# Attention scores of a fused recurrence, mixture and MLP kernel: three split products or one plain fp32 product

## The chip, the core and the metric

The kernel runs on one core of one Trainium2 chip. A core has a matmul engine (TensorE, PE in the profile; its loading of the stationary operand is listed apart as PEld), a vector engine (VectorE, DVE), an engine for activations (ScalarE, ACT), a general engine (GpSimd, POOL) and one that only issues transfers (SyncE, SP). They run side by side, each through its own list of instructions in order, and wait for each other by semaphores. SBUF is the working memory with 128 rows (partitions); matmul results go to PSUM, which has eight banks per partition. The metric is the time of one execution on the device in microseconds; the median of three runs is given.

## The reference

Three stages on a batch of 4 sequences of 768 positions. First a gated linear recurrence with 8 heads of 48:

```
state = alpha[:, :, t, :, None] * state + einsum('bhd,bhe->bhde', k[:, :, t], v[:, :, t])
y[:, :, t] = einsum('bhd,bhde->bhe', q[:, :, t], state)
```

Then causal attention with four experts, of which each position uses the two with the largest gate:

```
for e in range(E):                        # E = 4, Hd = 64
    q = x @ wq[e]; k = x @ wk[e]; v = x @ wv[e]
    scores = 1.0 / np.sqrt(Hd) * (q @ k.transpose(0, 2, 1))
    scores = np.where(causal, -1000000000.0, scores)
    a = softmax(scores)
    out += gate weight of e * (a @ v @ wo[e])
```

Last a layer norm and an MLP of width 384 to 1536 to 384 with a residual: `x + relu(xn @ w_ch1) @ w_ch2`. All in fp32. The weights of queries and keys are large (scaled by 23), so scores need many correct digits.

## The kernel before

**Numbers.** Two kinds of float are used on TensorE. A plain fp32 tile (F32) is multiplied by an instruction pair: one matmul call leaves two records in the trace. A tile of type FR (float32r) is multiplied by one record per call, with fewer digits. Where the kernel needs fp32 accuracy with FR tiles, it splits a value in a high part, rounded to FR by a ScalarE copy, and a low part, the rest, made on VectorE, and adds three products: high by high, low by high and high by low. The projections (line 304, 318), the output projection (505) and the MLP (631, 648) do so, and so do the attention scores (432). The recurrence (lines 221, 230, 244, 263), the transposes of the softmax (464) and the sums over values (487, 490) use plain fp32 operands.

**Stages.** `front()` walks over 24 chunks of 128 positions (6 per sequence): `gla_a`, `gla_b` and `gla_c` compute the recurrence, and after every second chunk `qkv(m)` projects 256 positions to queries, keys, values and gates. For queries and keys its matmuls fill a bank P with two row blocks of 128 x 256 (experts 0 and 1 in block 0, experts 2 and 3 in block 1, 64 rows each). The attention consists of 48 units (b, i, p): sequence b, query tile i of 128 positions, expert pair p. `scores(u)` makes the scores of the two experts of a pair (called heads here, h = 0 and 1) into PSUM, takes the row maximum (VectorE, line 438 and 440) and the exponential (ScalarE, line 442). Head h uses rows 64h to 64h+63 of TensorE's array, so that the two heads' matmuls are on different row tiles. A unit has 128 (i + 1) keys; above 512 it is worked in two halves of equal width, each with a bank per head. `transp(u)` transposes the exponentials, `av(u)` multiplies by the values, `wout` by the output weights. `back()` is the MLP in 12 blocks.

**Order.** The main loop goes over the units, makes scores two units ahead (LA = 2) and fills the gaps with steps of `front()` for sequences 0 to 2 and of `back()` for sequence 3, by tables of expected costs. The framework then orders each engine's list by its own schedule, so that one changed instruction can shift others. PSUM tiles are all named F and come from one pool of eight banks, handed out in turn.

**What is stored.** `new_gen(b)` makes, for even and odd b, four FR tiles of 128 x 2 x 768 (QH, QL, KH, KL: high and low parts of queries and keys) and the values V and gate weights W. The lines that the change touches are the copies after the projection (307 to 311) and the matmuls in `scores`:

```
for x in range(npc):
    for n, (qt, kt) in enumerate(((QH, KH), (QL, KH), (QH, KL))):
        for h in range(2):
            pe.matmul(P[h][x], qt[rs[h], p, qs], kt[rs[h], p, pw * x:pw * x + pw], ...)
```

Of the kernel before, what the change touches and what calls it, by code (L numbers as in the profile page):

```python
# [10 lines left out]
F32 = mybir.dt.float32  # L11
FR = mybir.dt.float32r
# [3 lines left out]
AF = mybir.ActivationFunctionType  # L16
OP = mybir.AluOpType
# [38 lines left out]
B, H, S, D = 4, 8, 768, 48  # L56
# [10 lines left out]
def f(ap):  # L67
    return ap.bitcast(F32)
# [3 lines left out]
def kernel(ctx: ExitStack, tc: tile.TileContext, akq, vd, wqkv, wo, g_ln, w1, w2, out):  # L72
    nc = tc.nc
    pe, dve, act, pool, sp = nc.tensor, nc.vector, nc.scalar, nc.gpsimd, nc.sync
# [21 lines left out]
    def psf():  # L96
        return psF.tile([128, 512], F32, tag="F", name="F")
# [16 lines left out]
    def new_gen(b):  # L114
        p = gen_pool[b % 2]
        if (b % 2, "t") not in GEN:
            GEN[b % 2, "t"] = (*(p.tile([128, 2, S], FR, name=f"{n}{b % 2}") for n in ("QH", "QL", "KH", "KL")),
                               p.tile([128, NSC, E * HD + E], F32, name=f"V{b % 2}"),
                               p.tile([128, NSC, E], F32, name=f"W{b % 2}"))
        GEN[b] = GEN[b % 2, "t"]  # L120
# [5 lines left out]
    GEN = {}  # L126
    wraw = []
    for k in range(KT):
        t = aw.tile([128, 772], F32, name="A", bufs=NA)
# [10 lines left out]
    for _ in range(NWU // 4):  # L140
        P = psf()
# [148 lines left out]
    def qkv(m):  # L290
        b, w = divmod(m, 3)
        if w == 0:
            new_gen(b)
        QH, QL, KH, KL, V, W = GEN[b]
        xh, xl = XT.pop(m)
        ts = slice(256 * w, 256 * w + 256)
        for mt in range(4):
            if mt % 2 == 0:
                P = psf().rearrange("p (x t) -> p x t", x=2)
            n = 0  # L300
            cs = slice(128 * mt, 128 * mt + 128)
            for wt, x in ((WH, xh), (WL, xh), (WH, xl)):
                for k in range(KT):
                    pe.matmul(P[:, mt % 2], wt[:, k, cs], x[:, k], start=(n == 0), stop=(n == 8))  # L304
                    n += 1
            if mt == 1:
                act.activation(QH[:, :, ts], P, AF.Copy, scale=0.125)
                dve.scalar_tensor_tensor(QL[:, :, ts], P, 0.125, f(QH[:, :, ts]), op0=OP.mult, op1=OP.subtract)
            elif mt == 3:
                act.activation(KH[:, :, ts], P, AF.Copy)  # L310
                dve.tensor_tensor(KL[:, :, ts], P, f(KH[:, :, ts]), op=OP.subtract)
            yield 980
        for t in range(2):
            P = psf()[:, :260]
            n = 0
            for wt, x in ((WH, xh), (WL, xh), (WH, xl)):
                for k in range(KT):
                    pe.matmul(P, x[:, k, 128 * t:128 * t + 128], wt[:, k, 512:772], start=(n == 0), stop=(n == 8))  # L318
                    n += 1
            act.activation(V[:, 2 * w + t], P, AF.Copy)  # L320
            yield 1000
        lg = V[:, 2 * w:2 * w + 2, 256:260]
        mx = sm.tile([128, 2, 1], F32, name="mx")
        dve.tensor_reduce(mx, lg, axis=AX.X, op=OP.max)
        l2 = sm.tile([128, 2, 4], F32, name="l2")
        pool.tensor_tensor(l2, lg, mx.to_broadcast([128, 2, 4]), op=OP.subtract)
        ex = sm.tile([128, 2, 4], F32, name="ex")
        act.activation(ex, l2, AF.Exp)
        rank = sm.tile([128, 2, 4], F32, name="rank")
        l_o = lg[:, :, None, :].to_broadcast([128, 2, 4, 4])  # L330
        l_s = lg[:, :, :, None].to_broadcast([128, 2, 4, 4])
        gt_ = sm.tile([128, 2, 4, 4], F32, name="gt_")
        eq_ = sm.tile([128, 2, 4, 4], F32, name="eq_")
        dve.tensor_tensor(gt_, l_o, l_s, op=OP.is_gt)
        dve.tensor_tensor(eq_, l_o, l_s, op=OP.is_equal)
        pool.tensor_tensor(eq_, eq_, tri[:, None].to_broadcast([128, 2, 4, 4]), op=OP.mult)
        pool.tensor_tensor(gt_, gt_, eq_, op=OP.add)
        dve.tensor_reduce(rank, gt_, axis=AX.X, op=OP.add)
        dve.scalar_tensor_tensor(ex, rank, 1.5, ex, op0=OP.is_lt, op1=OP.mult)
        sd = sm.tile([128, 2, 1], F32, name="sd")  # L340
        dve.tensor_reduce(sd, ex, axis=AX.X, op=OP.add)
        dve.tensor_scalar(sd, sd, 1e-9, None, op0=OP.add)
        dve.reciprocal(sd, sd)
        dve.tensor_tensor(W[:, 2 * w:2 * w + 2], ex, sd.to_broadcast([128, 2, 4]), op=OP.mult)
        yield 0
# [65 lines left out]

    def scores(u):
        b, i, p = UN[u]
        QH, QL, KH, KL, V, W = GEN[b]
        nk = 128 * (i + 1)
        qs = slice(128 * i, 128 * i + 128)
        nm = sm.tile([128, 2], F32, name="nm")
        den = sm.tile([128, 2], F32, name="den")
        M["nm"] = nm
        A = [aw.tile([128, 772], F32, name="A", bufs=NA) for _ in range(2)]  # L420
        wide = nk > 512
        pw = nk // 2 if wide else nk
        P = [[psf()[:, :pw] for x in range(1 + wide)] for h in range(2)]
        if wide:
            mx2 = sm.tile([128, 2], F32, name="mx2")
            dn2 = sm.tile([128, 2, 2], F32, name="dn2")
        npc = 1 + wide
        rs = [slice(64 * h, 64 * h + 64) for h in range(2)]
        for x in range(npc):
            for n, (qt, kt) in enumerate(((QH, KH), (QL, KH), (QH, KL))):  # L430
                for h in range(2):
                    pe.matmul(P[h][x], qt[rs[h], p, qs], kt[rs[h], p, pw * x:pw * x + pw], start=(n == 0), stop=(n == 2),  # L432
                              skip_group_check=True)
        for h in range(2):
            for x, t in enumerate(P[h]):
                m = mx2[:, h:h + 1] if x < npc - 1 else nm[:, h:h + 1]
                if x < npc - 1:
                    dve.tensor_reduce(m, t, axis=AX.X, op=OP.max, negate=True)
                else:
                    dve.tensor_tensor_reduce(t, t, cmask[:, 512 - pw:], -1.0, mx2[:, h:h + 1] if wide else 3e38, OP.add, OP.min, m)  # L440
            for x, t in enumerate(P[h]):
                act.activation(A[h][:, pw * x:pw * x + pw], t, AF.Exp, bias=nm[:, h:h + 1], scale=1.0 if x < npc - 1 else -1.0,  # L442
                               accum_out=dn2[:, h, x:x + 1] if wide else den[:, h:h + 1])
        AA[u] = A
        if wide:
            dve.scalar_tensor_tensor(den, dn2[:, :, 0], 1e-9, dn2[:, :, 1], op0=OP.add, op1=OP.add)
        else:
            dve.tensor_scalar(den, den, 1e-9, None, op0=OP.add)
        dve.reciprocal(den, den)
        rr = sm.tile([128, 2], F32, name="rr")  # L450
        pool.tensor_tensor(rr, den, W[:, i, 2 * p:2 * p + 2], op=OP.mult)
        RR[u] = rr
# [18 lines left out]

    def av(u):
        b, i, p = UN[u]
        V = GEN[b][4]
        if p == 0:
            OT[u // 2] = (aw.tile([128, 2, 128], FR, name="oh", bufs=2), aw.tile([128, 2, 128], FR, name="ol", bufs=2))
        oh, ol = OT[u // 2]
        P = psf()
        rr = RR.pop(u)
        at = ATT.pop(u)  # L480
        O = P[:, 128:256]
        with tc.manual_schedule(engines={mybir.EngineType.PE}):
            for x in range(i + 1):
                for h in range(2):
                    e = 2 * p + h
                    c = 128 * (h * (i + 1) + x)
                    pe.matmul(O[64 * h:64 * h + 64, :], V[:, x, HD * e:HD * e + HD], at[:, c:c + 128],  # L487
                              start=(x == 0), stop=(x == i), skip_group_check=True)
            for h in range(2):
                pe.matmul(P[64 * h:64 * h + 64, :128], rr[:, h:h + 1].to_broadcast([128, 64]), ident, start=True, stop=True,  # L490
                          skip_group_check=True)
        rb = aw.tile([128, 128], F32, name="rb", bufs=2)
        act.activation(rb, P[:, :128], AF.Copy)
        dve.tensor_tensor(rb, O, rb, op=OP.mult)  # L494
        act.activation(oh[:, p], rb, AF.Copy)
        (dve if OLE else pool).tensor_tensor(ol[:, p], rb, f(oh[:, p]), op=OP.subtract)
# [215 lines left out]
    for u in range(LA):  # L712
        scores(u)
    for u in range(nu):
        b, i, p = UN[u]
# [18 lines left out]
        else:  # L734
            nc2 = min(NC2, (u - u3) * CR // 2)
            while prog["cv"] < NC1 + nc2:
                n = prog["cv"]
# [84 lines left out]
```

## Time and profile before

| what | value |
|---|---|
| median of 3 runs | 748.21 us (744.76, 748.21, 753.51) |
| span of the profiled execution | 749.8 us |
| its mean granted TensorE clock | 0.97 of full speed |
| busy: TensorE, its weight loads | 713.5 us, 643.2 us |
| busy: VectorE, ScalarE, GpSimd | 447.5 us, 308.5 us, 174.5 us |
| records of the score matmuls (line 432) | 384, busy 51.2 us |

No time of the profiled execution apart from its span is given, so the span stands for it; it lies 1.6 us above the median. Busy is the time in which an engine had at least one instruction under way. Records of TensorE overlap, so its busy time, and the duration of one record, is more than what one instruction costs in a row of many; that is read from the distance between starts. The program has three parts that matter here: to about 60 us it starts up, from 60 to 360 us recurrence, projections and attention are mixed, from 360 to 462 us the attention of the last sequence is mixed with the MLP, and the rest is MLP alone.

### The profile page before, as it was taken

The page shows a single profiled execution, that of the slowest core. Times are in us where ns is not written, and L with a number is a line of the kernel's source. Part 1 is how long each engine was busy: PE and PEld are TensorE (multiplying, and loading weights), DVE is VectorE, ACT ScalarE, POOL GpSimd, SP SyncE. Part 2 cuts the span into 40 slices and gives each one's busy share as a digit, 9 for nine tenths or more (in the row PEclk, how much of TensorE's full clock was granted, in tenths as well). Part 3 has the DMA queues.
Part 4 walks back from the last instruction along what each step waited for, and adds up shares of the span by engine and source line. Part 5 has one row for each costly group of instructions (what it writes and reads, how often), then busy time and mean ns, then how long its engine had stood idle before and what let it go on. Part 6 is the DMA issues. An engine that isn't in the chain of part 4 may idle for free.

```text
span 749.8 us, 16242 instructions
## 1 busy us (share of the span) xinstructions
PE 713.5 (95%) x6520; PEld 643.2 (86%) x6520; DVE 447.5 (60%) x1241; ACT 308.5 (41%) x879; POOL 174.5 (23%) x284
## 2 busy tenths in 40 slices
PE   7599799989989999999899999999999999999998
PEld 6488678868868788779678888999999999999997
DVE  6757787767897787766678954254245335433521
ACT  3324455545555555555567545232223123212310
POOL 4624345243464334321223221000000000000000
PEclk8688999999999999999999999999999999999999
DMA  8113424233322622211932311001100100110100
GB/s 338 71 57 115 151 68 138 98 117 121 121 97 96 208 61 83 77 41 54 323 99 79 96 43 55 22 32 43 43 11 33 43 22 22 43 43 12 32 22 22
DMA packets 30427, 60.87 MB, mean 81 GB/s; under 512 B 2960, under 2 KB 19856, under 8 KB 30352
## 3 DMA queue, kind: packets, MB, share of 16 engines
q1 hardware_dynamic: 18864, 45.68, 18.3%
q10 hardware_dynamic: 8352, 9.44, 3.6%
q0 software_dynamic: 3136, 4.72, 2.3%
q8 instruction: 51, 0.84, 0.5%
q14 instruction: 24, 0.20, 0.1%
HBM read 45.67 MB, written 14.16 MB: 80 GB/s over the span
## 4 chain that ended last, share of the span: by engine, by line
PE 69%; DVE 9%; DMA 7%; ACT 4%; POOL 3%; issue 3%; SPq 0%; ACTq 0%; POOLq 0%; DVEq 0%
PE F L631 21%; PE F L648 20%; PE F L304 5%; PE F L487 5%; PE F L432 4%; PE F L464 3%; DMA ld<-in_akq_dram 3%; PE F L505 2%; DMA raw<-in_w_dram 2%; DVE gt L199 2%; PE F L263 2%; PE F L318 2%; PE F L221 1%; ACT A L442 1%; PE F L244 1%
## 5 line engine op out<-in xcount | busy, mean ns | idle before, releaser
L635 ACT ACTIVATE hh<-F 128x256 fp32r<-128x256 f32 x144 | 55.0, 384 | 196.6 <-PE F L631 196.0
L631 PE MATMUL F<-nh,w1hl 128*128 128x256 f32 x864 | 129.0, 284 | 0.0
L631 PEld LDWEIGHTS F<-nh,w1hl 128*128 128x128 f32 x864 | 114.4, 191 | 1.7 <-issue 0.7
L648 PE MATMUL F<-w2h,hh 128*128 128x384 f32 x288 | 98.8, 343 | 0.0
L648 PE MATMUL F<-w2l,hh 128*128 128x384 f32 x288 | 97.0, 337 | 0.0
L648 PE MATMUL F<-w2h,hl 128*128 128x384 f32 x288 | 96.9, 336 | 0.0
L636 DVE SCALAR_TENSOR_TENSOR hl<-F,hh 128x256 fp32r<-128x256 f32 x144 | 60.1, 419 | 56.8 <-ACT hh L635 56.3
L442 ACT ACTIVATE A<-F,nm 128x384 f32<-128x384 f32 (+4 forms) x128 | 68.4, 541 | 52.7 <-DVE nm L440 44.4
L652 DVE TENSOR_TENSOR xt<-F,xt 128x384 f32<-128x384 f32 x24 | 13.4, 558 | 110.5 <-PE F L648 110.5
L631 PE MATMUL F<-nl,w1hl 128*128 128x256 f32 x432 | 75.5, 283 | 0.0
L487 PE MATMUL F<-at,V 128*64 128x128 f32 x672 | 62.1, 286 | 2.3 <-ACT at L467 1.6
L631 PEld LDWEIGHTS F<-nl,w1hl 128*128 128x128 f32 x432 | 62.2, 192 | 0.2 <-issue 0.2
L487 PEld LDWEIGHTS F<-at,V 128*64 128x64 f32 x672 | 41.5, 137 | 19.1 <-issue 7.5
L464 PE MATMUL F<-ident,A 128*128 128x128 f32 x336 | 54.5, 284 | 3.3 <-DVE rb L494 2.6
L648 PEld LDWEIGHTS F<-w2h,hh 128*128 128x128 f32 x288 | 54.2, 188 | 1.1 <-issue 0.8
L648 PEld LDWEIGHTS F<-w2l,hh 128*128 128x128 f32 x288 | 54.2, 188 | 0.2
L648 PEld LDWEIGHTS F<-w2h,hl 128*128 128x128 f32 x288 | 54.1, 188 | 0.2 <-issue 0.2
L464 PEld LDWEIGHTS F<-ident,A 128*128 128x128 f32 x336 | 37.9, 142 | 12.6 <-issue 5.0
L221 PE MATMUL F<-ld 48*128 48x128 f32 x384 | 37.8, 309 | 9.1 <-issue 5.1
L221 PEld LDWEIGHTS F<-ld 48*128 48x128 f32 x384 | 30.2, 203 | 15.4 <-issue 9.8
L206 POOL TENSOR_TENSOR ld<-ld,gt 128x512 f32<-128x512 f32 (+1 forms) x26 | 30.2, 1166 | 56.4 <-DVE gt L199 29.1
L467 ACT ACTIVATE at<-F 128x512 f32<-128x512 f32 (+1 forms) x72 | 38.7, 542 | 6.6 <-PE F L464 4.8
(185 smaller groups left out, 1420.9 us busy)
## 6 DMA issues: line engine op xcount, KB each, us to landing
ld<-in_akq_dram SPq DMA_DIRECT2D x24, 770.0 KB, 4.8
vb<-in_vd_dram SPq DMA_DIRECT2D x24, 256.0 KB, 2.8
raw<-in_w_dram SPq DMA_DIRECT2D x18, 256.0 KB, 2.7
wsc<-whl ACTq DMA_DIRECT2D x18, 256.0 KB, 2.4
xs<-xo ACTq DMA_DIRECT2D x24, 192.0 KB, 1.9
w1hl<-wsc POOLq DMA_DIRECT2D x4, 1152.0 KB, 14.9
xt<-xs SPq DMA_DIRECT2D x24, 192.0 KB, 2.5
raw<-in_w_dram SPq DMA_DIRECT2D x12, 384.0 KB, 3.2
```

What stands on the lines that cost most here:

```text
L206: (dve if GQ else pool).tensor_tensor(q[:, js], q[:, js], gt[:, js, 1:], op=OP.mult)
L221: pe.matmul(P[h][:, j], k[r, j], q[r, j], start=True, stop=True)
L304: pe.matmul(P[:, mt % 2], wt[:, k, cs], x[:, k], start=(n == 0), stop=(n == 8))
L432: pe.matmul(P[h][x], qt[rs[h], p, qs], kt[rs[h], p, pw * x:pw * x + pw], start=(n == 0), stop=(n == 2), skip_group_check=True)
L442: act.activation(A[h][:, pw * x:pw * x + pw], t, AF.Exp, bias=nm[:, h:h + 1], scale=1.0 if x < npc - 1 else -1.0, accum_out=dn2[:, h, x:x ...
L464: pe.transpose(P[:, 128 * n:128 * n + 128], A[h][:, 128 * x:128 * x + 128], ident)
L467: act.activation(at[:, cs], P[:, :128 * len(g)], AF.Copy)
L487: pe.matmul(O[64 * h:64 * h + 64, :], V[:, x, HD * e:HD * e + HD], at[:, c:c + 128], start=(x == 0), stop=(x == i), skip_group_check=True)
L631: pe.matmul(P, w[:, k, c], x[:, k], start=(n == 0), stop=(n == 8))
L635: act.activation(hh, P, AF.Relu)
L636: dve.scalar_tensor_tensor(hl, P, 0.0, f(hh), op0=OP.max, op1=OP.subtract)
L648: pe.matmul(P, x[:, o], w[:, ff], start=(ff == 0 and n == 0), stop=(ff == KF - 1 and n == 2))
```

## The change

Queries and keys are kept as one plain fp32 tile each. The ScalarE copies out of PSUM stay (that of the queries with its factor 0.125); the two VectorE operations that made low parts are gone; `scores` issues one plain fp32 matmul per head and half where it issued three FR matmuls. Line numbers behind it move up by two or three.

```
-            GEN[b % 2, "t"] = (*(p.tile([128, 2, S], FR, name=f"{n}{b % 2}") for n in ("QH", "QL", "KH", "KL")),
+            GEN[b % 2, "t"] = (*(p.tile([128, 2, S], F32, name=f"{n}{b % 2}") for n in ("Q", "K")),
...
             if mt == 1:
-                act.activation(QH[:, :, ts], P, AF.Copy, scale=0.125)
-                dve.scalar_tensor_tensor(QL[:, :, ts], P, 0.125, f(QH[:, :, ts]), op0=OP.mult, op1=OP.subtract)
+                act.activation(Q[:, :, ts], P, AF.Copy, scale=0.125)
             elif mt == 3:
-                act.activation(KH[:, :, ts], P, AF.Copy)
-                dve.tensor_tensor(KL[:, :, ts], P, f(KH[:, :, ts]), op=OP.subtract)
+                act.activation(K[:, :, ts], P, AF.Copy)
...
         for x in range(npc):
-            for n, (qt, kt) in enumerate(((QH, KH), (QL, KH), (QH, KL))):
-                for h in range(2):
-                    pe.matmul(P[h][x], qt[rs[h], p, qs], kt[rs[h], p, pw * x:pw * x + pw], start=(n == 0), stop=(n == 2),
-                              skip_group_check=True)
+            for h in range(2):
+                pe.matmul(P[h][x], Q[rs[h], p, qs], K[rs[h], p, pw * x:pw * x + pw], start=True, stop=True,
+                          skip_group_check=True)
```

The order of the instructions changes with it. First, TensorE in the first sequence, query tile 5, first expert pair (768 keys in two halves of 384). In these rows stand line, operation, result and operands (with the number of the buffer), size and, after x, how many calls follow in a row; a plain fp32 call is one row here and two records in a trace. Before:

```order
L263 MATMUL F<-smk,vb_87 32x128 x4
L263 MATMUL F<-ld_84,st_91 32x128 x4
L432 MATMUL F<-KH_375,QH_373 128x384 x2
L432 MATMUL F<-KH_375,QL_374 128x384 x2
L432 MATMUL F<-KL_376,QH_373 128x384 x2
L432 MATMUL F<-KH_375,QH_373 128x384 x2
L432 MATMUL F<-KH_375,QL_374 128x384 x2
L432 MATMUL F<-KL_376,QH_373 128x384 x2
L263 MATMUL F<-smk,vb_87 32x128 x4
```

The same place on TensorE with the change (line 429 is the former 432):

```order
L263 MATMUL F<-smk,vb_87 32x128 x4
L263 MATMUL F<-ld_84,st_91 32x128 x4
L429 MATMUL F<-K_374,Q_373 128x384 x3
L263 MATMUL F<-smk,vb_87 32x128
L429 MATMUL F<-K_374,Q_373 128x384
L263 MATMUL F<-smk,vb_87 32x128 x3
```

Twelve calls became four, and one matmul of the recurrence (line 263) now stands between the third and the fourth, so that the two heads of one half are no longer neighbours.

Second, VectorE at the projection of the second positions of sequence 1. Line 225 masks scores of the recurrence, 204 and 205 scale its keys, 469 (466 with the change) copies transposed exponentials, 494 scales the output. Before:

```order
L225 TENSOR_TENSOR smk<-F,gmask 128x512
L449 RECIPROCAL den<-den 128x2
L311 TENSOR_TENSOR KL_1410<-F,KH_1409 128x2x256
L225 TENSOR_TENSOR smk<-F,gmask 128x512
L204 TENSOR_TENSOR ld_83<-ld_83,gi 128x512
L494 TENSOR_TENSOR rb<-F,rb 128x128
L469 COPY at<-F 128x512
```

VectorE at this place with the change:

```order
L446 RECIPROCAL den<-den 128x2
L225 TENSOR_TENSOR smk<-F,gmask 128x512
L204 TENSOR_TENSOR ld_83<-ld_83,gi 128x512
L225 TENSOR_TENSOR smk<-F,gmask 128x512
L205 SCALAR_TENSOR_TENSOR ld_83<-ld_83 128x512
L466 COPY at<-F 128x512
```

The low part of the keys has left the queue, and a step of the recurrence (line 204) has moved one place up. Third, TensorE in the last sequence, query tile 4 (640 keys in two halves of 320). Line 464 (461 with the change) transposes, 487 (484) multiplies by the values. Before:

```order
L464 MATMUL F<-ident,A 128x128 x4
L432 MATMUL F<-KH_1409,QH_1407 128x320
L432 MATMUL F<-KH_1409,QL_1408 128x320
L432 MATMUL F<-KL_1410,QH_1407 128x320
L487 MATMUL F<-at,V_377 64x128 x4
L432 MATMUL F<-KH_1409,QH_1407 128x320
L432 MATMUL F<-KH_1409,QL_1408 128x320
L432 MATMUL F<-KL_1410,QH_1407 128x320
```

This place on TensorE with the change:

```order
L461 MATMUL F<-ident,A 128x128 x4
L429 MATMUL F<-K_1368,Q_1367 128x320
L484 MATMUL F<-at,V_375 64x128 x4
L429 MATMUL F<-K_1368,Q_1367 128x320 x3
L461 MATMUL F<-ident,A 128x128 x8
```

One head's half stands alone ahead of the values' matmuls in both orders, and the rest of the unit's scores follows behind them.

## Rows read from the trace of the kernel before

**Rows 1.** The page's table of engines: busy us (share of the span) and instructions.

```profile
PE 713.5 (95%) x6520; PEld 643.2 (86%) x6520; DVE 447.5 (60%) x1241; ACT 308.5 (41%) x879; POOL 174.5 (23%) x284
```

**Rows 2.** Stretches: their us, then PE, PEld, DVE, ACT, POOL busy us; PE clock.

```profile
60.00:360.00 300.00, 286.23 (x3266) 239.80 (x3266) 226.51 (x627) 155.23 (x445) 118.67 (x197) 0.97 0.30 101
360.00:462.00 102.00, 98.53 (x807) 80.68 (x803) 74.62 (x242) 58.82 (x185) 25.26 (x43) 0.98 0.42 121
```

**Rows 3.** Line 432 by itself: durations min/median/max in ns, starts, forms.

```profile
L432 PE MATMUL F<-KH,QH x128: 301/412/771, 59.5 to 458.5; 64*128 64x384 f32 x48, 64*128 64x320 f32 x32, 64*128 64x128 f32 x16, 64*128 64x256 f32 x16
```

**Rows 4.** Timeline, pairs of score records: start us, us merged, what, xcount.

```profile
178.92 0.28 PE L432 MATMUL F<-KH,QL 64*128 64x128 f32 x2
179.03 0.28 PE L432 MATMUL F<-KL,QH 64*128 64x128 f32 x2
...
204.16 0.34 PE L432 MATMUL F<-KH,QL 64*128 64x384 f32 x2
204.34 0.34 PE L432 MATMUL F<-KL,QH 64*128 64x384 f32 x2
...
209.41 0.40 PE L432 MATMUL F<-KH,QL 64*128 64x512 f32 x2
209.65 0.40 PE L432 MATMUL F<-KL,QH 64*128 64x512 f32 x2
...
240.77 0.31 PE L432 MATMUL F<-KH,QL 64*128 64x320 f32 x2
240.91 0.31 PE L432 MATMUL F<-KL,QH 64*128 64x320 f32 x2
...
297.02 0.28 PE L432 MATMUL F<-KH,QL 64*128 64x256 f32 x2
297.14 0.28 PE L432 MATMUL F<-KL,QH 64*128 64x256 f32 x2
```

**Rows 5.** Timeline, first and last of 38 score records without a companion.

```profile
150.96 0.33 PE L432 MATMUL F<-KH,QH 64*128 64x384 f32 x1
...
435.67 0.38 PE L432 MATMUL F<-KL,QH 64*128 64x256 f32 x1
```

**Rows 6.** Plain fp32: page's costliest groups, timeline, and two lines' weight loads.

```profile
L221 PE MATMUL F<-ld 48*128 48x128 f32 x384 | 37.8, 309 | 9.1 <-issue 5.1
...
177.08 1.16 PE L221 MATMUL F<-ld 48*128 48x128 f32 x16
178.17 0.65 PE L230 MATMUL F<-ident,ld 128*128 128x128 f32 x4
...
207.07 1.06 PE L244 MATMUL F<-vb,kt 128*128 128x128 f32 x8
207.97 0.27 PE L464 MATMUL F<-ident,A 128*128 128x128 f32 x1
...
210.44 0.62 PE L263 MATMUL F<-smk,vb 128*32 128x128 f32 x16
210.88 0.40 PE L263 MATMUL F<-ld,st 112*32 112x128 f32 x8
...
L263 PEld LDWEIGHTS F<-smk,vb x768: 106/109/178, 18.8 to 329.0; 128*32 128x32 f32 x192
...
L244 PEld LDWEIGHTS F<-vb,kt x160: 186/192/337, 16.7 to 316.8; 128*128 128x128 f32 x160
```

**Rows 7.** Lines 308 and 311 on VectorE: durations in ns, starts, forms.

```profile
L308 DVE SCALAR_TENSOR_TENSOR QL<-F,QH x12: 677/691/692, 44.0 to 351.1; 128x512 fp32r<-128x512 f32 x12
...
L311 DVE TENSOR_TENSOR KL<-F,KH x12: 664/687/692, 46.5 to 353.3; 128x512 fp32r<-128x512 f32 x12
```

**Rows 8.** Timeline from 124 to 143 us: two low parts and a wait.

```profile
124.70 0.69 DVE L308 SCALAR_TENSOR_TENSOR QL<-F,QH 128x512 fp32r<-128x512 f32 x1
...
135.06 0.67 DVE L311 TENSOR_TENSOR KL<-F,KH 128x512 fp32r<-128x512 f32 x1
...
142.86 0.62 PE L505 MATMUL F<-OWH,oh 128*128 128x384 f32 x2 [0.80 <-ACT A L442]
```

More of the change, by code (lines that the diff above doesn't have):

```diff
@@ L293, in qkv @@
             new_gen(b)
-        QH, QL, KH, KL, V, W = GEN[b]
+        Q, K, V, W = GEN[b]
         xh, xl = XT.pop(m)
@@ L413, in scores @@
         b, i, p = UN[u]
-        QH, QL, KH, KL, V, W = GEN[b]
+        Q, K, V, W = GEN[b]
         nk = 128 * (i + 1)
@@ L473, in av @@
         b, i, p = UN[u]
-        V = GEN[b][4]
+        V = GEN[b][2]
         if p == 0:
```

## The prediction

> **What bounds the kernel now.** I read the page's table of engines first: TensorE counts as busy for 95% of the span, VectorE for 60%, ScalarE for 41% [rows 1]. The table by stretches then shows where the changed code lives. From 60 to 360 us, where recurrence, projections and attention are interleaved, TensorE is busy for 286.2 of 300 us and VectorE for 226.5; from 360 to 462, where attention is interleaved with the MLP, for 98.5 and 74.6 of 102 [rows 2]. So TensorE is the bound all along, with 13.8 us of idleness in the first of these stretches and 3.5 us in the second. VectorE is a strong second there: three quarters full, and often in the way. After 462 us there are no scores and nothing changes.
>
> Since a busy TensorE is not one at its peak, I priced its instructions by the distance from one start to the next, not by the duration in the row.
>
> **Scores before.** Each of the 48 units makes scores for two heads. A unit with more than 512 keys works in two halves, so there are 64 pieces: 8 each of 128, 256, 384 and 512 keys (query tiles 0 to 3), and 16 each of 320 and 384 (tiles 4 and 5). The records agree: the first of the three products has 128, two heads for each of 64 pieces, in these widths [rows 3]. The two heads use rows 0 to 63 and 64 to 127 of the array, and the timeline merges their two records into one row (x2): they run side by side. From one pair to the next it is 0.11 us at 128 columns, 0.12 at 256, 0.14 at 320, 0.18 at 384 and 0.24 at 512 [rows 4]. Three pairs a piece give 8 x 3 x (0.11 + 0.12 + 0.18 + 0.24) + 16 x 3 x (0.14 + 0.18) = 15.6 + 15.4 = 31.0 us. Not all run in pairs: 38 of the 384 records (24 at 320 columns, 12 at 384, 2 at 256; the first and the last are shown) run alone, 19 more steps than needed [rows 5]. That is 12 x 0.14 + 6 x 0.18 + 0.12 = 2.9 us. Sum before: **33.9 us** of TensorE.
>
> **Scores after.** The price of a plain fp32 matmul stands in other lines of this trace. The 192 calls at line 221 (two heads, four pairs, 24 chunks) leave 384 records [rows 6]: one call is two records. At line 244 (full array) eight records of 128 columns take from 207.07 to 207.97, 0.112 us each [rows 6]. Line 221 is built like the scores, two row tiles side by side: 16 records from 177.08 to 178.17, less some 0.2 us for entering and leaving the tiled mode (which the scores pay today too), are eight steps of 0.111 us, so two row tiles overlap in plain fp32 as well [rows 6]. What sets this 0.11 us? It could be the loading of the stationary operand, since at 128 columns even the scores of today, one record a product, step by 0.11 [rows 4]. Line 263 speaks against that: its weights are 32 columns wide and load in 109 ns instead of 192, and still 16 records, four at a time, take 0.44 us, 0.11 a step [rows 6]. I therefore take the 0.11 us as the time of streaming 128 columns, in proportion to the width: 0.333 us a step at 384 columns, against 0.18 today. Two steps a piece for 21,504 columns in all 64 pieces (8 x 1280 + 16 x 704) are 168 x 0.222 = 37.3 us. In the new order on TensorE seven pieces (three of 384, two of 320, two of 256) have their heads separated by other work and run one after the other, 2,304 columns twice: 18 x 0.222 = 4.0 us. Sum after: **41.3 us**, or **+7.4 us** on the engine that bounds. The lower end is the price of today's steps, two instead of three (second rival); the upper end is two heads that never overlap, 37.3 + 37.3 - 33.9 = +41 us.
>
> By the Trainium skill, "FP8 and Floating Point Precision", section TensorE Precision Notes, a true fp32 product takes four passes through the array; two records at twice the column time, as read above, are just that. By the same skill's "Perfetto Trace Analysis", section Engine Utilization (note on the tensor core's rate), the low-and-high form of fp32 halves the output rate, which would be two passes; the sum by that is the second rival's, and line 263's steps speak against it.
>
> **What is taken off VectorE.** The 12 low parts of the queries (691 ns) and the 12 of the keys (687 ns) are gone: 24 x 0.69 = 16.5 us of VectorE, nearly all of it in the stretch from 44 to 354 us [rows 7]. That is worth time only where TensorE waits for VectorE. One place shows it: around 124.7 and 135.1 us both low parts stand in a VectorE queue that hardly pauses, and at 142.86 TensorE waits 0.80 us for an exponential that waits for the row maximum at the end of that queue [rows 8]. Taking 1.36 us out of the queue removes this wait. Of the other 13 us of idleness in the stretch I give it a tenth, 1.2 us, because the rest of the work is in order behind transfers and ScalarE: **-2.0 us**, bounds 0 and -7 (half of the idleness). The matmuls of a later product no longer wait for low parts, which costs nothing today: scores are issued many microseconds after them. What is late next at these places is the exponential itself.
>
> **What is moved, and what costs nothing.** The two ScalarE copies per projection stay, only their output type differs; ScalarE is busy for 155 of 300 us [rows 2], so that even a few microseconds there would be covered, and without the cover a slower copy would delay only scores issued much later. PSUM banks of the projection come free 0.69 us earlier. Banks of the scores fill more slowly at 320 columns and more, while VectorE's read of them is often queued anyhow; part of the longer matmuls falls into time in which TensorE now waits (in the middle of the unit at 150 us, where one head runs alone, among others): **-0.8 us**, bounds 0 and -2. No queue of transfers changes. Two tiles less per generation shift the MLP's memory to the front; TensorE idles 3.5 us in all between 360 and 462 us [rows 2], so this is worth at most that, either way, and I take 0.
>
> **Sum.** 7.4 - 2.0 - 0.8 = +4.6 us. The profiled execution spans 749.8 us, 1.6 above the median of the three runs, 748.2, so I expect a span of some 754.4 and a median of **752.8 us**. The three runs of before spread from 744.8 to 753.5; about 1%, 7.5 us, is what a measurement can tell from no change, so this forecast is called no change though I expect it to be slightly slower.
>
> **Rivals.**
> First, VectorE was the hidden bound: its 16.5 us come back as half of TensorE's idleness, 7 us. For it: VectorE 75% busy, exponentials waiting for maxima. Against it: TensorE has only 13.8 us to give there, and much of that follows transfers and ScalarE. Time 748.2 + 7.4 - 0.8 - 7 = 747.8.
> Second, a plain fp32 record streams as fast as one of today's, and 0.11 us is only a floor at 128 columns. Then two records replace three: 20.7 us for the pieces and 2.1 for the seven separated ones, 22.8 against 33.9, and with VectorE's 2.0 the time is 748.2 - 11.1 - 2.0 = 735.1. For it: no plain fp32 record in the trace is wider than 128 columns. Against it: line 263.
> Third, slower: the heads of more pieces run one after the other, since one head's PSUM bank is still unread when the other's is ready, and a plain fp32 piece then pays two long steps again. Today it happens to the unit at 150 us [rows 5]. One of the 57 adjacent pieces costs (37.3 - 4.0) / 57 = 0.58 us; five of them decide, 752.8 + 2.9 = 755.7 being slower by 1%. With 15 it is 761.6. For it: each bank is written more slowly and so held longer. Against: VectorE empties banks sooner.
>
> **How the numbers follow.** Forecast 0.60, first rival 0.15, second 0.08, third 0.17. Faster by over 1% (below 740.7) holds the second rival and a little of the first: 0.10. Slower by over 1% (above 755.7) holds nearly all of the third and a quarter of the forecast, whose terms add up to 756 to 758 where VectorE gives nothing back: 0.31. Within 1%: 0.59. The range reaches from 742, which takes in the first rival and a fast run, to 762, where the third stands with 15 pieces; the second rival and the far part of the third are left out.
>
> **What would show it.** In the profile of the changed kernel the score line has 256 records, two steps a piece, of 0.33 us at 384 columns and 0.44 at 512; steps of 0.18 and 0.24 would mean the second rival, and records merged as x1 rather than x2 in many pieces the third. Lines 308 and 311 have no heir on VectorE, whose busy time falls by 16 us; TensorE's idleness from 60 to 360 us should shrink by some 3 us and the wait at 142.86 be gone. If TensorE's idleness falls by much more, the first rival is right. The forecast is wrong altogether if another order of the instructions, which the change brings with it at many places, opens waits that no row here shows.

## The result, and the profile after

The changed kernel takes 754.4 us (median of 14 runs, 748.8 to 759.4) against 748.5 (14 runs): a ratio of 1.0075, 95% interval 1.0049 to 1.0101, that is 5.6 us slower (3.7 to 7.6). The forecast was 752.8 us, 4.6 slower, and no change by the 1% bound.

The page of the changed kernel, its engines (answers to [rows 1]):

```profile
span 752.5 us, 15956 instructions
PE 715.7 (95%) x6392; PEld 629.0 (84%) x6392; DVE 431.6 (57%) x1217; ACT 309.1 (41%) x879; POOL 172.5 (23%) x284
```

VectorE lost 15.9 us and 24 instructions, TensorE 128 records, and the span still grew by 2.7 us. Spans compare only with spans: this execution took 754.5 us with a span of 752.5, and the listed executions of the kernel before take 1.7 us more than their spans. The profiled execution before, with its span of 749.8, was therefore some 3 us slower than the median of its kernel, which is why the spans differ by less than the medians. The same stretches as in [rows 2], columns as there:

```profile
60.00:360.00 300.00, 287.68 (x3148) 229.46 (x3146) 209.29 (x589) 153.72 (x436) 115.92 (x194) 0.98 0.31 100
360.00:462.00 102.00, 98.07 (x753) 75.57 (x752) 73.45 (x238) 58.38 (x181) 24.98 (x44) 1.00 0.41 122
```

TensorE's idleness from 60 to 360 us went from 13.8 to 12.3 us, from 360 to 462 from 3.5 to 3.9: 17.2 us before, 16.3 after. The forecast had some 3 us less in the first stretch; it is 1.5, and half a microsecond more in the second.

The score line by itself (as [rows 3]), and three places of the timeline where the scores stand in the midst of other tiled matmuls, so that nothing is spent on entering the mode: 128, 384 and 512 columns.

```profile
L429 PE MATMUL F<-K,Q x256: 270/482/1057, 56.5 to 461.5; 64*128 64x384 f32 x48, 64*128 64x320 f32 x32, 64*128 64x128 f32 x16, 64*128 64x256 f32 x16
...
104.88 1.03 PE L429 MATMUL F<-K,Q 64*128 64x512 f32 x4
105.83 0.55 PE L230 MATMUL F<-ident,ld 128*128 128x128 f32 x3
...
265.85 1.46 PE L429 MATMUL F<-K,Q 64*128 64x384 f32 x8
267.24 0.44 PE L230 MATMUL F<-ident,ld 128*128 128x128 f32 x2
...
275.90 0.39 PE L429 MATMUL F<-K,Q 64*128 64x128 f32 x4
276.13 0.39 PE L221 MATMUL F<-ld 48*128 48x128 f32 x4
```

Four records of 128 columns, two steps, take 0.23 us: 0.11 a step. Eight of 384, four steps, take 1.39, of which some 0.1 is spent on leaving the mode: 0.32 a step. Four of 512 take 0.95, less 0.1: 0.43. That is 0.84 ns a column, twice the 0.42 ns of one column a cycle at 2.4 GHz, the level granted at all three places. The kernel before, at the same unit of sequence 1 (two halves of 384, three products each):

```profile
263.80 0.42 PE L432 MATMUL F<-KH,QH 64*128 64x384 f32 x2
264.06 0.33 PE L432 MATMUL F<-KH,QL 64*128 64x384 f32 x2
264.24 0.34 PE L432 MATMUL F<-KL,QH 64*128 64x384 f32 x2
264.41 0.34 PE L432 MATMUL F<-KH,QH 64*128 64x384 f32 x2
264.59 0.35 PE L432 MATMUL F<-KH,QL 64*128 64x384 f32 x2
264.76 0.35 PE L432 MATMUL F<-KL,QH 64*128 64x384 f32 x2
265.04 0.55 PE L230 MATMUL F<-ident,ld 128*128 128x128 f32 x3
```

The last pair takes 0.28 us to the next instruction, where the others step by 0.17 to 0.18: that is the 0.1 us of leaving the mode. From 263.80 to 265.04 it is 1.24 us for six steps, against 1.39 for four after: two pieces cost 0.15 us more. The first step before takes 0.26 us, 0.08 more than the rest, so the steps by themselves differ by more: 4 x 0.32 against 6 x 0.175, 0.23 us. Summed over all places, from the first score record of a place to the next instruction on TensorE, the scores take 48.3 us before and 54.3 after, **6.1 us more**, entering and leaving included, and waits too: 1.6 us before and 0.7 after. Without the waits the difference is 7.0 us. Of 256 records 40 have no record of the other head that starts with them (38 of 384 before): 24 of 384 columns, 8 of 320, 4 each of 512 and 256.

The wait of 0.80 us in [rows 8] is gone; at the same matmul (now line 502, first row) none is listed. Others of its kind stand elsewhere; the longest is in the second row:

```profile
141.67 0.51 PE L502 MATMUL F<-OWH,oh 128*128 128x384 f32 x2
...
258.47 0.63 PE L502 MATMUL F<-OWH,oh 128*128 128x384 f32 x2 [2.23 <-ACT A L439]
```

Part of what became of VectorE's time shows in its own list of waits (engine, what, whom it waited for: total us, times, longest), of the changed kernel:

```profile
DVE rb L491 <- ACT rb L490: 16.6, 16, 2.7
...
DVE F L437 <- PE F L429: 11.6, 10, 3.3
```

The row maximum (line 437) waits 11.6 us for the scores; before, the same line 440 waited 4.8 us for them, and the scaling of the output 10.1 us instead of 16.6. These two waits grew by 13.3 us together.

### The profile page after: what moved, and what is told of

Its sections match the earlier page's. It is cut to its first block, busy times and chain, and to the rows that moved or that the text cites. A ratio compares the mean times of both kernels' runs of the same rounds, so it can differ in the third digit from the quotient of the medians.

```text
span 752.5 us, 15956 instructions
## 1 busy us (share of the span) xinstructions
PE 715.7 (95%) x6392; PEld 629.0 (84%) x6392; DVE 431.6 (57%) x1217; ACT 309.1 (41%) x879; POOL 172.5 (23%) x284
## 4 chain that ended last, share of the span: by engine, by line
PE 66%; DMA 2%; DVE 2%; ACT 1%; issue 0%; SPq 0%; ACTq 0%; DVEq 0%
PE F L628 21%; PE F L645 20%; PE F L484 5%; PE F L429 4%; PE F L461 3%; PE F L304 3%; PE F L502 2%; PE F L263 2%; PE F L316 2%; DMA raw<-in_w_dram 1%; PE F L221 1%; PE F L608 1%; DMA ld<-in_akq_dram 1%; PE F L487 1%; PE F L244 1%; ACT A L439 0%
## 5 line engine op out<-in xcount | busy, mean ns | idle before, releaser
L429 PE MATMUL F<-K,Q 64*128 64x384 f32 (+4 forms) x256 | 58.4, 497 | 1.7 <-ACT A L439 0.9
```

Of the source, the lines that this page charges most:

```text
L429: pe.matmul(P[h][x], Q[rs[h], p, qs], K[rs[h], p, pw * x:pw * x + pw], start=True, stop=True, skip_group_check=True)
```

## The experiments

**Low parts put back.** The changed kernel, with VectorE's work of before; the two tiles are never read.

```
...
                 act.activation(Q[:, :, ts], P, AF.Copy, scale=0.125)
+                dve.scalar_tensor_tensor(QL[:, :, ts], P, 0.125, Q[:, :, ts], op0=OP.mult, op1=OP.subtract)
...
                 act.activation(K[:, :, ts], P, AF.Copy)
+                dve.tensor_tensor(KL[:, :, ts], P, K[:, :, ts], op=OP.subtract)
```

Expected:

> The changed kernel (754.4 us) with the 24 VectorE operations for low parts put back: they write two tiles that nobody reads. TensorE's score work is that of the change, VectorE's that of before. Theory (TensorE is the bound, taking 16.5 us off VectorE gave back about 2 us): 756.4 us, 1.0 to 1.1% above the kernel before. Rival (VectorE is a hidden bound and its relief gave back 7 us or more): 761 us or more, 1.7% above. Nothing given back at all: 754.4 us. VectorE busy rises from 431.6 to 447.5 us, TensorE idle from 60 to 360 us from 12.3 to some 14 us by the theory, to 19 by the rival.

Measured: 754.4 us, 1.0071 of before (1.0046 to 1.0096), the same as the changed kernel without them. VectorE is busy again for 447.4 us, and TensorE idles 14.3 us from 60 to 360:

```profile
60.00:360.00 300.00, 285.69 (x3126) 228.88 (x3126) 220.77 (x606) 152.86 (x432) 113.13 (x192) 0.97 0.30 100
360.00:462.00 102.00, 100.15 (x764) 76.61 (x761) 74.68 (x243) 58.26 (x181) 26.12 (x45) 1.00 0.42 123
```

The 2.0 us more from 60 to 360 are 2.1 less from 360 to 462. Against the changed kernel it is 0.3 us less, give or take 2.7, by the two intervals: the rival's 7 us are excluded, and the forecast's 2.0 are not excluded by this run alone. As this kernel differs from the one before in TensorE's scores alone (and in the order that follows from them), it also gives their price by itself: 0.71% of 749.2 us, 5.3 us (3.4 to 7.2). Its scores' places take 53.5 us, 5.2 more than before.

**No low parts, three products of high parts.** The other side of the same question: TensorE's records are those of before, VectorE's work that of the change.

```
-                dve.scalar_tensor_tensor(QL[:, :, ts], P, 0.125, f(QH[:, :, ts]), op0=OP.mult, op1=OP.subtract)
...
-                dve.tensor_tensor(KL[:, :, ts], P, f(KH[:, :, ts]), op=OP.subtract)
...
-            for n, (qt, kt) in enumerate(((QH, KH), (QL, KH), (QH, KL))):
+            for n, (qt, kt) in enumerate(((QH, KH),) * 3):
```

Expected:

> The kernel before (748.5 us) without low parts: no VectorE operations for them, and all three products of the scores are high by high, so TensorE issues the same 384 score records. It leaves out the low parts and triples the scores. Theory: VectorE's relief alone is worth 2 us, 746.5 us, 0.3% below before, hard to tell from nothing. Rival (VectorE a hidden bound): 741 us or less, 1% below.

Measured: 1.0003 of before (0.9973 to 1.0032), VectorE busy 432.6 us. No gain shows; one of over 2.0 us lies outside the interval, so the forecast's 2.0 is at its very edge. Together with the first run, where putting the work back moved the time by -0.04%, the best value is about zero, and 2.0 is unlikely.

**Every score matmul twice.** The changed kernel with the loop over products back, now with the same operands.

```
-                act.activation(Q[:, :, ts], P, AF.Copy, scale=0.125)
+                act.activation(Q[:, :, ts], P, AF.Copy, scale=0.0625)
...
         for x in range(npc):
-            for h in range(2):
-                pe.matmul(P[h][x], Q[rs[h], p, qs], ..., start=True, stop=True, ...)
+            for n in range(2):
+                for h in range(2):
+                    pe.matmul(P[h][x], Q[rs[h], p, qs], ..., start=(n == 0), stop=(n == 1), ...)
```

Expected:

> The changed kernel with every score matmul issued twice into the same bank (queries scaled by 1/16 instead of 1/8, so that the sum is the same). It adds the whole price of the plain fp32 scores once more: 37.3 us for the pairs and 4 to 6 us for pieces whose heads run apart, some 42 us of TensorE. Theory (score time on TensorE counts in full): 754.4 + 42 = 796 us, 1.063 of before, from 790 to 800. Rival (added TensorE time falls into waits, at half price): 775 us, 1.036. Steps at 384 columns are 0.32 us in either case.

Measured: 804.1 us, 1.0732 (1.0685 to 1.0778), 49.7 us above the changed kernel, more than either number. The scores' places on TensorE grew from 54.3 to 94.7 us, 40.4, close to the 42 expected. Some 5 us of the other 9.3 are new waits late in the attention, one above all:

```profile
PE F L462 <- ACT A L440: 5.2, 1, 5.2
PE F L629 <- ACT A L440: 1.4, 1, 1.4
```

From 360 us to the end of the attention TensorE idles 9.0 us instead of 3.9. The granted clock is lower as well: 0.96 instead of 0.98 from 60 to 360 us, and 0.94 from 360 to 480 us, where the changed kernel had 1.00 from 360 to 462. How much of the 4 us that remain comes from it is not shown. Score time counts in full, and the rival's half price falls.

**One product.** The kernel before with high by high alone and no low parts.

```
...
-            for n, (qt, kt) in enumerate(((QH, KH), (QL, KH), (QH, KL))):
+            for n, (qt, kt) in enumerate(((QH, KH),) * 1):
...
```

Expected:

> The kernel before with one product (high by high) and no low parts, 128 score records instead of 384. It leaves out two of three products, so scores are less exact. TensorE loses two thirds of 33.9 us, 22.6 us, VectorE 16.5 us. Theory: 748.5 - 22.6 - 2.0 = 724 us, 0.967 of before; if the time of entering the tiled mode counts per unit and stays, no less. Rival (what TensorE gives up goes into waits for VectorE and ScalarE, at half price): 735 us, 0.982.

Measured: 724.6 us, 0.968 (0.9634 to 0.9726), 24.6 us below before. The scores' places took 22.8 us instead of 48.3, 25.4 less. The run with three products of high parts, which has no low parts either, differs in the two products alone: 25.4 us of time and 26.6 us at the places. So downward, too, a microsecond of scores is a microsecond of the kernel, and VectorE's relief adds nothing that shows.

**Low parts three times.** What more work on VectorE does to the kernel before:

```
                 act.activation(QH[:, :, ts], P, AF.Copy, scale=0.125)
-                dve.scalar_tensor_tensor(QL[:, :, ts], P, 0.125, f(QH[:, :, ts]), ...)
+                dve.scalar_tensor_tensor(QL[:, :, ts], P, 0.125, f(QH[:, :, ts]), ...)
+                dve.scalar_tensor_tensor(QL[:, :, ts], P, 0.125, f(QH[:, :, ts]), ...)
+                dve.scalar_tensor_tensor(QL[:, :, ts], P, 0.125, f(QH[:, :, ts]), ...)
```

and the same for the keys. Expected:

> The kernel before with each of the 24 low parts made three times over, so that VectorE has 48 operations of 0.69 us, 33 us, more to do; nothing else changes and the output is the same. The theory after the first four runs (TensorE's score time counts in full, the 16.5 us on VectorE counted for nothing, because its time there is covered): the first added 16.5 us cost nothing much and the second little, 749 to 753 us, up to 0.5% above before. Rival (VectorE has no room upwards, so that its relief would be worth something in a kernel with less TensorE work): a quarter or more of the 33 us shows, 757 us or more, 1.1% above.

Measured: 1.0048 (1.0019 to 1.0077), 3.6 us (1.4 to 5.8) for 33 us of VectorE, a ninth. From 60 to 360 us VectorE stands at 247.5 and TensorE's idleness at 17.3 instead of 13.8 us, but from 360 to 462 TensorE idles 0.5 instead of 3.5:

```profile
60.00:360.00 300.00, 282.74 (x3221) 234.63 (x3220) 247.54 (x651) 151.43 (x433) 115.35 (x193) 0.98 0.30 99
360.00:462.00 102.00, 101.51 (x832) 83.47 (x831) 78.10 (x253) 61.70 (x191) 27.77 (x47) 1.00 0.43 125
```

That is 17.8 us of idleness against 17.2 in both together, and the profiled execution is the fastest of this kernel (749.7 us), so the trace does not show where the 3.6 us are. By the times VectorE's cover is not endless, but it ends above today's load: more work costs a little, less gives nothing that these runs can tell.

**Heads kept together.** The kernel before, with the order of the program fixed for a unit's score matmuls on TensorE.

```
...
-        for x in range(npc):
+        with tc.manual_schedule(engines={mybir.EngineType.PE}):
+            for x in range(npc):
...
```

Expected:

> The kernel before with the score matmuls of a unit kept in the order of the program on TensorE, which leaves 14 records out of 384 without a companion of the other head, where 38 are alone before. Theory (score time on TensorE counts in full): 12 steps of 0.14 to 0.18 us less, some 1.8 us, 747.4 us, 0.2% below before, hardly to be told from nothing. Rival (keeping the order makes TensorE wait for the second head's bank): the same or slower, 749 us or more.

Measured: 0.9991 (0.9962 to 1.0019), 748.7 against 749.9 us. The interval, 2.8 us less to 1.4 more, holds the gain expected and nothing as well. In the trace 24 records are still alone, where the order had 14: a record also loses its companion when the second head's bank comes free late, as at 153 us, where TensorE waits 1.9 us for ScalarE. The scores' places took 47.2 us, 1.0 less than before. No version tried with the full computation is clearly faster than the kernel before.

## Why the prediction was right, step by step

**The price of plain fp32 was read rightly.** The step that decided was the reading of 0.11 us for 128 columns as streaming time and not as a floor: 0.32 us at 384 columns, where the forecast said 0.333 and the second rival 0.18. So the second rival is out. The argument for it was weaker than it reads: the weight loads of line 263 last 109 ns, which is the step itself, so they do not rule out that loading sets it. What does is the wider records, whose loads are as short as before (186 against 183 ns at the median) while their steps grow with the width. Two row tiles do overlap in plain fp32 (x4 and x8 in one row of the timeline, two records starting within 0.01 us).

**The sum on TensorE was about right, with two errors that run against each other.** Forecast +7.4 us; the trace has +6.1 at the scores' places, +7.0 without the waits that fall into them, and the runs with VectorE's work held equal +5.3 (3.4 to 7.2). Steps of wider records are a little shorter than in proportion to 0.111 us at 128 columns, 0.32 and 0.43 instead of 0.333 and 0.444: 3 to 4% of 37.3 us, some 1.3 us less. But ten pieces, not seven, have records that run alone. At the measured steps (0.21 at 256 columns and 0.27 at 320, by the starts of the records) their 20 extra steps are at most 12 x 0.32 + 4 x 0.27 + 2 x 0.43 + 2 x 0.21 = 6.2 us, where the forecast had 4.0; near 220, 250 and 371 us the heads' records start 0.14 to 0.43 us apart and overlap in part, so it is less than that.

**The granted clock hid part of the price.** The 46 executions of the kernel before that are listed with the experiments had a mean granted clock of 0.9735, the 14 of the changed kernel 0.978; in the profiled ones the difference is largest up to 60 us, 0.79 against 0.86. Fitted over all listed executions, one with 0.01 more of clock is 5.2 us shorter. By this estimate, at the same clock, the change costs 7.3 us (give or take 0.9), the low parts put back change that by 0.0, leaving them out of the kernel before gives 0.9 (give or take 0.9), one product gives 22.4, and low parts three times cost 4.7. That is close to the forecast's 7.4 on TensorE and leaves its other two terms near nothing. No run holds the clock fixed, so whether its rise came with the change or by chance stays open.

**The relief of VectorE was mis-sized.** The term of -2.0 us measured about 0 in two runs made for it, each to within 2 to 3 us. Its one row, the wait at 142.86, did vanish, but that was no gain: waits of the same kind stand elsewhere, 16.3 us of idleness in all against 17.2. The forecast scaled a wait that it could see to a tenth of those that it could not; in the experiments the others do not hang on those 16.5 us to any extent that shows. VectorE spends much of them waiting, for the scores (4.8 us before, 11.6 after) and for ScalarE at the scaling of the output (10.1 and 16.6). That is not the longer scores alone: without low parts, but with three products, these waits are 8.8 and 16.4 us. The first rival is out.

**The absorption (-0.8 us)** cannot be told from nothing: the doubled scores cost more than their own time, not less, and the single product gave back all but 0.8 us of what its places lost. The errors of the three terms partly cancel: 7.4 - 2.0 - 0.8 = 4.6, measured 5.6, against some 5.3 to 7.0 on TensorE and, as far as the runs can tell, nothing else. That 4.6 lies so near 5.6 is partly luck: two terms for which no run shows anything took off 2.8 us, and the higher clock of the changed kernel's executions took off, by the estimate above, some 2. The 756 to 758 that the prediction gives for its terms where VectorE gives nothing back does not follow from them: 748.2 + 7.4 is 755.6.

**The third rival came true in small part only.** The records without a companion are 40 of 256 instead of 38 of 384, ten pieces where the forecast had seven, three of the five more that would have decided. In steps that is one more than before (20 against 19), though each is nearly twice as long. The order of the program, which separates the heads of seven pieces, told only a part of them. One of the others, near 150 us, is where the second head's bank was late (TensorE's waits from 60 to 360 us in the changed kernel):

```profile
PE F L429 <- ACT at L464: 0.7, 1, 0.7
```

For the rest the reason is not shown.

## What to carry to other kernels

Where an engine bounds, count its steps, not its instructions: 256 records instead of 384 were slower because each takes some 0.84 ns a column where the others take 0.46 (at 384 and 512 columns), and 24 operations off the second busiest engine, three quarters full, were worth nothing that could be measured. Compare the granted clock of the executions as well as their times: here, by the estimate above, it moved by enough to hide a quarter of the price. Price an operand type at the width at which it will be used, and where the trace has it at one width only, look for a neighbour with another weight width to tell streaming from a floor, and check that its weight loads are shorter than the step. A single wait that the change removes is no estimate of what it gives back, as long as the engine that waited is the bound at the next instruction as well.

## What the runs showed of the hardware that was not expected

A plain fp32 matmul cost four column times at every width read above: two records of 0.11, 0.32 and 0.43 us for 128, 384 and 512 columns at a granted clock of 1.00, where one column time is 0.42 ns. By the Trainium skill, "FP8 and Floating Point Precision", section TensorE Precision Notes, a true fp32 product takes four passes, and these runs agree with it. By the Trainium skill, "Perfetto Trace Analysis", section Engine Utilization, the low-and-high form of fp32 halves the rate; read as the rate of the whole product, that gives an estimate of 0.16 us a record at 384 columns, and these runs show 0.32. Three separate products of the reduced type were thus cheaper than the one exact product (1.24 against 1.39 us for the unit of 768 keys above), except at 128 columns, where both have steps of 0.11 us and two are fewer than three.
